# A new order table for the same 2,900 operations of a fused convolution and linear-attention kernel

## The chip, the cores and the metric

The kernel runs on one core of a Trainium2 chip. The metric is the device time of one execution in microseconds (us), the median of a few runs. Its engines are TensorE (PE in the profile, with its weight loads as PEld), VectorE (DVE), ScalarE (ACT), GpSimd (POOL) and SyncE (SP). SP issues all data transfers of this kernel.

## The reference, cut to what matters

Two independent layers are computed and laid side by side in the last axis. `u` and `x` are (1, 2048, 576).

```python
# left half: a state-space convolution per channel, N = 128 states
dt = exp(log_dt); A = -exp(log_A_real) + 1j * A_imag; C = (C_real + 1j * C_imag) * dt[:, None]
K  = 2 * einsum("dn,dnl->dl", C, exp((A * dt[:, None])[:, :, None] * arange(2048))).real
a  = irfft(rfft(u_t, 4096) * rfft(K, 4096))[:, :, :2048] (transposed back) + u * D_skip
# right half: linear attention, 32 heads of 18
q, k, v = split(x @ wqkv)
phi(z)  = concat(softmax(z @ w_phi), softmax(-(z @ w_phi)))      # per head
num = phi(q) @ (phi(k)^T v);  den = phi(q) . sum(phi(k))
b = (num / (den + 1e-6)) @ wo
out = concat([a, b], -1)
```

## The kernel before, in words

The kernel is written in two layers. `body` first describes the work: each call of `op` records one operation with its engine, a cost, the function that emits its instructions, and the buffers that it reads and writes. 2,900 operations are recorded; 486 of them are PE blocks of 1 to 32 matmuls, 366 are transfers. Then `Plan.run(ORDER)` goes through a table of numbers and emits the operations in the table's order. The table is the only thing that decides in which order each engine meets its instructions; nothing reorders them on the chip. An engine works through its own instructions in that order and stops at the first one whose inputs, or whose buffer, are not there yet.

One entry of the table is an operation's number with marks behind it. `1494` is operation 1494. `376*` says that the operation goes to its second engine: copies from PSUM can go to ACT or DVE, and many SBUF-to-SBUF operations to POOL or DVE. `/3/0/5` are the slots that its new buffers take: 8 PSUM banks (`ps`), 14 large buffers (`zi`, `ac`, `x9`, `e`, `ks`, `E`), 19 rows (`v1`, `o`, `ot`, `yo`, `ub`, `kb`, `us2`, `zo`, `ff`, `fT`, `mx`), 7 small ones, 2 each of `pi`, `mg`, `cs`. A buffer waits until the slot's former user has been read. `!` puts a tiny ACTIVATE in front, which loads the activation table early. `35+28` puts 28 matmuls with zeros ahead of operation 35.

The work itself, by the names in the functions:

- `fold` and `whole` (L504 to L536) prepare weights: `wh` is the rounded part, `wl` the rest, so that three products of reduced precision make up one in f32.
- `key_tile(t)`, 16 tiles of 128 rows: `load_x` (L547, L467) splits x into a rounded part and a rest, three `gemm`s of 14 matmuls give phi's argument and v, `softmax` (L590 to L607) works on DVE, POOL and ACT, and 32 small matmuls add to phi(k)^T v.
- `query_tile(t)`, 16 tiles: two `gemm`s, `softmax`, transposes (L705), the division by `den` (L724), transposes (L735, L736) and two `gemm`s with `wo`.
- `u_first(k)`, 16 steps, and `product(p, half)`, 16 steps, and `last`, 16 steps: the Fourier transform of u, its product with that of K, and the way back, all as small matmuls that use the array in tiles of 32 or 64 rows and columns (`ub,ff`, `kb,ff`, `ac,ff`, `zi,w`).
- `params(blk)`, 6 blocks (L843 to L886): angles, on vectors of 96 per partition, mostly on DVE. `phases` (L904, L908): chains of integer additions on POOL. `waves` (L918 to L926): sines on ACT. `group(g)`, 36 groups: exponentials (L942, L949), products on DVE (L953 to L959), 32 small matmuls (`E,cs`), then copies and sums into `ks`. `k_first` turns each quarter of the groups into `zi` and writes it to DRAM; before it, L471 adds D_skip to `ks` (`ks<-ks,dsk`).

L452 is the line of the helper that issues almost all matmuls, L457 and L460 are the copies from PSUM, L467 and L471 the binary operations, so one line stands for many uses, and the names of tiles tell them apart. `copy("any", ...)` is what makes an ACT-or-DVE choice possible:

```python
op(("act", "dve"), (c_act(n), c_dve(n)), lambda e: act.activation(dst(), src(), AF.Copy) if e == "act" else dve.tensor_copy(dst(), src()), r=r, w=w)
```

All stages overlap: key tiles, u steps and the first groups share the first 200 us, query tiles, groups and the first half of the products the next 150 us, and the last 150 us hold the other products, `last` and the remaining query tiles.

## Time and profile before

| what | value |
| --- | --- |
| runs | 515.43, 518.12, 514.73 us; median 515.43 us |
| the profiled execution | 511.75 us, of which 510.0 us are the span from the first to the last instruction |
| granted TensorE clock | 0.999 |
| transfers | 114.67 MB by 366 issues on SP, 225 GB/s of HBM over the span |
| ACT_TABLE_LOAD | 41, of 1.28 us each |

The profile takes one execution. A row of a timeline reads: start and length in us, engine, source line, instruction, tiles written and read, shape, count, and in brackets the engine's idle time before it with what ended it. A row of groups ends with the group's busy time, the mean length of one in ns, and the idle time before. Lengths of neighbouring DVE instructions overlap a little, since the end of one lies beside the start of the next.

### The profile page before, as it was taken

The page shows a single profiled execution, that of the slowest core. Times are in us where ns is not written, and L with a number is a line of the kernel's source. Part 1 is how long each engine was busy: PE and PEld are TensorE (multiplying, and loading weights), DVE is VectorE, ACT ScalarE, POOL GpSimd, SP SyncE. Part 2 cuts the span into 40 slices and gives each one's busy share as a digit, 9 for nine tenths or more (in the row PEclk, how much of TensorE's full clock was granted, in tenths as well). Part 3 has the DMA queues.
Part 4 walks back from the last instruction along what each step waited for, and adds up shares of the span by engine and source line. Part 5 has one row for each costly group of instructions (what it writes and reads, how often), then busy time and mean ns, then how long its engine had stood idle before and what let it go on. Part 6 is the DMA issues. An engine that isn't in the chain of part 4 may idle for free.

```text
span 510.0 us, 20296 instructions
## 1 busy us (share of the span) xinstructions
PE 496.6 (97%) x8436; PEld 412.6 (81%) x8436; DVE 457.5 (90%) x1013; ACT 396.8 (78%) x683; POOL 334.2 (66%) x403
## 2 busy tenths in 40 slices
PE   7999999999999999899999999999999999999996
PEld 7799888999998879697887866776788886667976
DVE  4999999999899999999999999998989879789774
ACT  4699787999879989979989889899896445454331
POOL 1645697788987997995994569796554455634400
PEclk9999999999999999999999999999999999999999
DMA  7985947715137586781687965468986997998797
GB/s 212 333 294 178 330 143 252 235 57 170 59 121 254 149 257 207 212 275 58 211 239 255 286 180 181 147 219 272 293 269 213 347 274 219 321 311 295 260 314 193
DMA packets 80511, 115.95 MB, mean 227 GB/s; under 512 B 12452, under 2 KB 57636, under 8 KB 80420
## 3 DMA queue, kind: packets, MB, share of 16 engines
q1 hardware_dynamic: 80420, 114.67, 71.1%
q8 instruction: 66, 1.08, 0.9%
q14 instruction: 25, 0.20, 0.1%
HBM read 65.63 MB, written 49.01 MB: 225 GB/s over the span
## 4 chain that ended last, share of the span: by engine, by line
PE 80%; DVE 7%; ACT 6%; POOL 2%; DMA 2%; issue 2%; SPq 0%; POOLq 0%; DVEq 0%
PE ps L452 75%; PE ps L705 3%; PE ps L735 2%; POOL cs L908 1%; ACT cs L918 1%; DVE E L471 1%; DMA xd<-x 1%; DMA ub<-dram 1%; ACT e L598 1%; DMA fT<-in_wphi_dram 1%; POOL o L601 1%; DVE wl L520 1%; DVE e L467 0%; DVE zi L457 0%; DVE small L602 0%
## 5 line engine op out<-in xcount | busy, mean ns | idle before, releaser
L452 PE MATMUL ps<-wh,x 128*128 128x288 f32 (+2 forms) x1008 | 240.2, 318 | 1.0 <-ACT wh L519 0.4
L452 PEld LDWEIGHTS ps<-wh,x 128*128 128x128 f32 x1008 | 173.0, 188 | 11.8 <-issue 2.8
L452 PE MATMUL ps<-wl,x 128*128 128x288 f32 (+2 forms) x560 | 175.0, 313 | 0.0
L452 PEld LDWEIGHTS ps<-wl,x 128*128 128x128 f32 x560 | 105.3, 188 | 1.2
L908 POOL TENSOR_TENSOR cs<-cs,pi 128x64 int32<-128x64 int32 (+4 forms) x90 | 91.9, 1022 | 5.5
L601 POOL TENSOR_TENSOR o<-e 128x576 f32<-128x576 f32 x32 | 42.4, 1330 | 28.8 <-ACT e L598 22.3
L467 POOL TENSOR_TENSOR E<-v,cs 128x512 f32<-128x512 f32 x31 | 39.5, 1290 | 15.5 <-ACT v L949 12.6
L471 DVE TENSOR_TENSOR ac<-us,ps 128x576 f32<-128x576 f32 x64 | 44.8, 747 | 3.5 <-PE ps L452 2.5
L953 DVE TENSOR_TENSOR cs<-ps,cs 128x1024 f32<-128x1024 f32 x36 | 43.7, 1214 | 2.8 <-ACT ps L942 2.4
L942 ACT ACTIVATE ps<-ps 128x512 f32<-128x512 f32 x72 | 41.6, 591 | 5.1 <-PE ps L452 4.8
L598 ACT ACTIVATE e<-e 128x1152 f32<-128x1152 f32 x32 | 37.4, 1168 | 7.0 <-POOL e L467 4.8
L452 PEld LDWEIGHTS ps<-E,cs 128*32 128x32 f32 x2304 | 34.3, 110 | 10.5 <-issue 5.7
L467 POOL TENSOR_TENSOR e<-small,e 128x576 f32<-128x576 f32 x27 | 31.7, 1173 | 15.7 <-DVE small L467 10.7
L452 PE MATMUL ps<-sel,mg 128*128 128x512 f32 x108 | 40.4, 439 | 1.4 <-DVE e L471 1.0
L452 PE MATMUL ps<-E,cs 128*32 128x64 f32 x2304 | 40.1, 220 | 1.4 <-issue 0.6
L926 ACT ACTIVATE cs<-cs,hp 128x1024 f32<-128x1024 f32 x36 | 40.4, 1141 | 0.0
L925 ACT ACTIVATE cs<-cs 128x1024 f32<-128x1024 int32 x36 | 37.0, 1054 | 0.3
L918 ACT ACTIVATE cs<-cs 128x2048 f32<-128x2048 int32 x18 | 34.4, 1912 | 2.6 <-POOL cs L908 2.5
L457 ACT ACTIVATE zi<-ps 128x288 f32<-128x288 f32 x79 | 28.1, 414 | 8.4 <-PE ps L452 8.4
L467 POOL TENSOR_TENSOR e<-e,small 128x576 f32<-128x576 f32 x25 | 29.7, 1189 | 7.3 <-DVE small L467 6.6
L890 POOL TENSOR_TENSOR pi<-pi 128x192 int32<-128x192 int32 (+1 forms) x42 | 20.0, 486 | 18.9 <-DVE pi L886 16.8
L467 POOL TENSOR_TENSOR ac<-ac 128x288 f32<-128x288 f32 x24 | 19.2, 825 | 18.8 <-DVE ac L471 8.8
(146 smaller groups left out, 1050.0 us busy)
## 6 DMA issues: line engine op xcount, KB each, us to landing
dram<-zi SPq DMA_DIRECT2D x32, 288.0 KB, 4.8
xd<-x SPq DMA_DIRECT2D x16, 576.0 KB, 4.7
dram<-zi SPq DMA_DIRECT2D x16, 576.0 KB, 5.2
x<-xd SPq DMA_DIRECT2D x16, 576.0 KB, 5.6
kb<-dram SPq DMA_DIRECT2D x32, 288.0 KB, 4.6
ub<-dram SPq DMA_DIRECT2D x32, 288.0 KB, 6.2
dram<-zo SPq DMA_DIRECT2D x32, 288.0 KB, 4.4
zi<-dram SPq DMA_DIRECT2D x16, 576.0 KB, 8.8
```

Of the source, the lines that this page charges most:

```text
L452: pe.matmul(o, l, r, start=start, stop=stop, skip_group_check=skip)
L457: op(("act", "dve"), (c_act(n), c_dve(n)), lambda e: act.activation(dst(), src(), AF.Copy) if e == "act" else dve.tensor_copy(dst(), src() ...
L467: op(eng, [c_dve(n[0]) if e == "dve" else c_pool(n[1]) for e in eng], lambda e: (dve if e == "dve" else pool).tensor_tensor(dst(), a(), b( ...
L471: op(eng, c_dve(n) if eng == "dve" else c_pool(n), lambda: e.tensor_tensor(dst(), a(), b(), op=alu), r=r, w=w, with_=with_, lock=eng == "p ...
L598: op("act", c_act(1152) + 40, lambda: act.activation(e.t, e.t, AF.Exp), r=[e], w=[e], table="exp")
L601: op("pool", c_pool(517), lambda: pool.tensor_tensor(pair.t, e.t[:, :, :, 0:9], e.t[:, :, :, 9:18], op=ALU.add), r=[e], w=[pair], lock=True)
L908: op("pool", c_add(4 * n * W), lambda n=n, j=j: pool.tensor_tensor(x()[:, :, :, n:2 * n], x()[:, :, :, 0:n], pi.t[:, j:j + 2, gs].bitcast( ...
L918: op(("act", "dve"), (c_act(n) + 45, c_dve(n)), lambda e: act.activation(cs.t[:, 0], x(), AF.Abs) if e == "act" else dve.scalar_tensor_ten ...
L925: op("act", c_act(64 * W) + 150, lambda at=at: act.activation(at(1), at(1).bitcast(I32), AF.Sin, scale=TURN), r=[cs], w=[sine], with_=[cs] ...
L926: op("act", c_act(64 * W) + 225, lambda at=at: act.activation(at(0), at(0), AF.Sin, scale=-TURN, bias=hp.t), r=[cs, hp, sine], w=[both], w ...
L942: op("act", c_act(512) + 12, lambda: act.activation(ps.t, ps.t, AF.Exp), r=[ps], w=[ps], table="exp")
L953: op("dve", c_dve(64 * W), lambda: dve.tensor_tensor(F(), both(M.t), F(), op=ALU.mult), r=[M, ready], w=[long], with_=[cs])
```

## The change

The table `ORDER` is replaced by another one. It holds the same 2,900 operations, and nothing else of the kernel differs. The new table is one line shorter, so that every line behind it has a number that is lower by one (L452 becomes L451). The first two lines of each:

```diff
 ORDER = """
-180/0 33 0/0 1 1353 3 1358 2 1360 1362 72/1 1361 1366 396/2 1365 1368 1367/3 1369 1370 1371 1372 4/4 35+28/0 1359 1373
-1374 126/5 1377 1363/0 1364 1375 1376 1378 1379/3 1380 1381 34/1 5/0 7/2 10 19/6 36 12/1 374/7 37 26/2 6/3 8 40/3 20/4
...
+2847 2848 2850 847 2880/2/0/6 1112 2849 1086 2868 2892 2873/7/5/7 2861 2869 2871 2881* 2882 2870 2883 2885 2894/3/4/14
+2895 2874 2852/0/1/2 1116/5/4 2884 2853* 2896 1117/10 849/1 2875 848/2 1118 1008 1119 1120 2876 2878 2897 850/6 2854
+2855 2898 2877 2856 2862 2863 2899 1121/3 2857 851 852 2864 1123/16 1122/1 1124 1125
```

In words, the new table is the former one with most entries moved by a few places. PE's blocks keep their places within a few blocks; the 28 matmuls with zeros stay. 172 operations change their engine: 63 from ACT to DVE, 57 from DVE to ACT, 27 from POOL to DVE, 25 from DVE to POOL. DVE's instructions go from 1,013 to 1,021, ACT's operations from 636 to 630, POOL's from 399 to 397. The changes of activation table in ACT's order go from 41 to 43, the early loads (`!`) from 6 to 8. The slots are dealt out anew.

Three places show it. The first is DVE near the start, where the weights' rests (`wl`) are made while the first key tile's x is split (`x<-zo,x`: the tile in f32 less its rounded part). Before:

```order
L622 MEMSET ps 128x288
L520 TENSOR_TENSOR wl<-ps,wh 128x4x126
L467 TENSOR_TENSOR x_216<-zo,x_216 128x512
L520 TENSOR_TENSOR wl<-ps,wh 128x126 x4
L520 TENSOR_TENSOR wl<-ps,wh 128x4x126
L520 TENSOR_TENSOR wl<-ps,wh 128x72
L536 TENSOR_TENSOR wl<-zi,wh 128x5x192
```

And now:

```order
L519 TENSOR_TENSOR wl<-ps,wh 128x4x126
L519 TENSOR_TENSOR wl<-ps,wh 128x126
L466 TENSOR_TENSOR x_240<-zo,x_240 128x512
L466 TENSOR_TENSOR x_240<-zo,x_240 64x128
L519 TENSOR_TENSOR wl<-ps,wh 128x4x126
L519 TENSOR_TENSOR wl<-ps,wh 128x126
L535 TENSOR_TENSOR wl<-zi,wh 128x5x192
```

The subtraction of 64x128, which stood on POOL, now stands on DVE ahead of the last two `wl`.

The second place is DVE around the addition of D_skip to the second quarter's `ks` (L471 before, L470 now; 128x36), behind which PE's second `k_first` can start. `ax`, `ay`, `mx`, `mn`, `cim` belong to `params`, the other `ks` to groups. Before:

```order
L859 SCALAR_TENSOR_TENSOR mx<-ax,ay 128x96
L471 TENSOR_TENSOR mn<-ax,ay 128x96
L471 TENSOR_TENSOR ay<-ay,ax 128x96
L457 COPY ks<-ps 128x32x4
L471 TENSOR_TENSOR x_4010<-ps,x_4010 64x128
L471 TENSOR_TENSOR ks<-ps,ks 128x32x4 x3
L471 TENSOR_TENSOR ks<-ks,dsk 128x36
L471 TENSOR_TENSOR ks<-ps,ks 128x32x4
L871 RECIPROCAL mx<-mx 128x96
```

And now:

```order
L855 TENSOR_SCALAR cim<-cim 128x96
L470 TENSOR_TENSOR ks<-ps,ks 128x32x4
L470 TENSOR_TENSOR ay<-ay,ax 128x96
L470 TENSOR_TENSOR ks<-ps,ks 128x32x4
L589 TENSOR_REDUCE small<-ps 128x16
L470 TENSOR_TENSOR ks<-ps,ks 128x32x4 x2
L470 TENSOR_TENSOR ks<-ks,dsk 128x36
L470 TENSOR_TENSOR ks<-ps,ks 128x32x4
L870 RECIPROCAL mx<-mx 128x96
```

Ahead of that addition stood 472 DVE instructions before, and 487 stand there now, while 196 PE blocks stand ahead of that `k_first` in both. The row of `mn`, which stood just ahead, now stands elsewhere, and a maximum of a softmax (`small<-ps`) has come in.

The third place is PE late in the program, where step `p1` of a product (`ub,ff`, 64x32 tiles of the array), its `p2` (`kb,ff`, 32x32 tiles) and a query tile's transposes (`ident,e`, the whole array) meet. Before:

```order
L452 MATMUL ps<-wl,x_7743 128x288
L452 MATMUL ps<-ub,ff 32x288 x16
L452 MATMUL ps<-kb,ff 32x288 x16
L705 MATMUL ps<-ident,e 128x128 x5
L452 MATMUL ps<-zi,w_432 64x288 x4
```

And now:

```order
L451 MATMUL ps<-wl,x_7750 128x288
L451 MATMUL ps<-ub,ff 32x288 x16
L704 MATMUL ps<-ident,e 128x128
L451 MATMUL ps<-kb,ff 32x288 x16
L704 MATMUL ps<-ident,e 128x128 x4
L451 MATMUL ps<-zi,w_2188 64x288 x4
```

One transpose moved between the two steps, so that the array's tiling changes once more often. Over the whole program it changes 219 times between neighbouring PE blocks before and 229 times now; behind the first 326 blocks it is 77 and 83.

## The prediction

> **What bounds the kernel now.** I read the windows by stage first, then the timelines of DVE and PE at the two borders between the stages, then the groups by line for prices. The columns of the windows are PE, PEld, DVE, ACT, POOL, the clock, the DMA share and GB/s.

> ```profile
> 20.00:231.00 211.00, 207.72 (x3444) 184.67 (x3442) 204.92 (x443) 188.70 (x300) 171.20 (x209) 1.00 0.63 200
> 231.00:348.00 117.00, 114.90 (x2224) 89.01 (x2225) 109.58 (x248) 106.05 (x178) 86.95 (x97) 1.00 0.66 205
> 348.00:510.00 162.00, 157.36 (x2670) 123.25 (x2668) 130.72 (x293) 91.03 (x184) 70.11 (x78) 1.00 0.86 274
> ```

> PE looks full everywhere, but its busy time includes ends that are modelled. DVE tells the stages apart. From 20 to 231 us it is busy 204.92 of 211 us, idle for 6.1 (2.9%); from 231 to 348 it is idle for 7.4 of 117 (6.3%); behind that for 31.3 of 162. So the first stage is DVE's, the second nearly so, and the third is PE's. I chose the borders where PE waits for DVE. The first is the second `k_first`, in DVE's and PE's timelines:

> ```profile
> 230.44 0.49 DVE L471 TENSOR_TENSOR ks<-ks,dsk 128x36 f32<-128x36 f32 x1
> 230.85 0.28 DVE L471 TENSOR_TENSOR ks<-ps,ks 128x128 f32<-128x128 f32 x1
> 231.05 0.74 DVE L871 RECIPROCAL mx<-mx 128x96 f32<-128x96 f32 x1
> 230.98 0.77 PE L452 MATMUL ps<-ks,w 32*128 32x288 f32 x8 [0.36 <-DVE ks L471]
> ```

> The addition of D_skip ends at 230.93, and PE, idle by then, starts 0.05 us later. No row of DVE here has an idle time in brackets: the addition came when DVE came to it, and DVE had 472 instructions ahead of it. The second border is the block `E,cs` of the sixteenth group:

> ```profile
> 347.63 0.68 DVE L959 SCALAR_TENSOR_TENSOR E<-ps,cs 128x512 f32<-128x512 f32 x1
> 348.37 1.46 PE L452 MATMUL ps<-E,cs 128*32 128x64 f32 x64
> ```

> The last `E` ends at 348.31, PE starts at 348.37, and 720 instructions of DVE stand ahead. What PE can do by those two points is thus set by the time of DVE's instructions ahead of them plus DVE's idle time. That is what I count for the new order.

> **DVE's additional work ahead of the borders.** In the new order 487 DVE instructions stand ahead of the first border, 15 more. Order alone moves one more ahead than behind, of lengths that cancel to nothing. The other 14 come from changed engines. Before that point 25 copies go from ACT to DVE and 16 back, and 17 operations from POOL to DVE and 12 back. The groups' mean lengths (in ns, the second number behind the bar) give their price:

> ```profile
> L457 DVE COPY zi<-ps 128x288 f32<-128x288 f32 x49 | 20.8, 451 | 4.4 <-PE ps L452 3.6 <-POOL small L467 0.4
> L457 DVE COPY v<-ps 128x180 f32<-128x180 f32 (+1 forms) x6 | 2.5, 411 | 0.1
> L457 DVE COPY ks<-ps 128x128 f32<-128x128 f32 x13 | 3.5, 278 | 0.8 <-PE ps L452 0.8
> L467 DVE TENSOR_TENSOR x<-zo,x 128x512 fp32r<-128x512 f32 (+1 forms) x20 | 13.4, 676 | 0.4 <-ACT x L547 0.2
> L467 DVE TENSOR_TENSOR kb<-ub 128x288 f32<-128x288 f32 x14 | 7.0, 503 | 0.0
> L467 DVE TENSOR_TENSOR small<-small 128x32 f32<-128x32 f32 x20 | 4.7, 240 | 0.1
> L467 DVE TENSOR_TENSOR e<-e,small 128x576 f32<-128x576 f32 x7 | 5.4, 773 | 0.0
> ```

> By net count: 2 copies of 128x288 at 0.451 (one into `zi`, one into `e`) 0.90; 5 copies of v at 0.411, 2.06; 2 copies of `ks` at 0.278, 0.56; 2 of `x<-zo,x` at 0.676, 1.35; 1 `kb` at 0.503; 3 `small` at 0.240, 0.72; and one `e<-e,small` less, −0.77. Together 5.3. The rows of DVE overlap: the one at 230.85 lasts 0.28, to 231.13, and the next starts at 231.05. At 0.07 to 0.08 for each of 14 that takes off 1.0, which leaves **4.3**. By the second border it is 737 instructions instead of 720, two more, small ones at 0.24, or 0.5: **+4.8 us** of DVE work ahead of it. The subtraction that the new order puts ahead of the last two `wl` in the head is one of the `x<-zo,x`, so it is counted; the nearest PE row is

> ```profile
> 15.36 0.41 PE L452 MATMUL ps<-wh,x 128*128 128x378 f32 x1 [0.37 <-ACT wh L519]
> ```

> and shows PE's first gemm waiting for these weights already.

> **DVE's idle time.** The order between the borders is new as well, and with it the 7.4 us of idle time. An order that hands DVE more may also leave it fewer gaps. The bounds are none absorbed and all: 7.4 here and 6.1 ahead of 231, 13.5. I take the value that the trace shows DVE to reach over a long stage, the 2.9% from 20 to 231 us: 2.9% of 117 is 3.4, so 7.4 − 3.4 = **4.0** are absorbed. Ahead of 231 nothing is, since that stage is at the 2.9% already.

> **Waits inside DVE's busy time.** Some of that time isn't work:

> ```profile
> 6.31 0.26 DVE L471 TENSOR_TENSOR mn<-mn,mx 128x96 f32<-128x96 f32 x1
> 232.38 1.98 DVE L471 TENSOR_TENSOR mn<-mn,mx 128x96 f32<-128x96 f32 x1
> 229.06 5.18 POOL L908 TENSOR_TENSOR cs<-cs,pi 128x64 int32<-128x64 int32 x5
> L471 DVE TENSOR_TENSOR mn<-mn,mx 128x96 f32<-128x96 f32 x6 | 3.2, 539 | 0.0
> 10.12 0.46 DVE L471 TENSOR_TENSOR pi<-pi,ot 128x288 f32<-128x288 f32 x1
> L471 DVE TENSOR_TENSOR pi<-pi,ot 128x288 f32<-128x288 f32 x6 | 4.1, 686 | 0.0
> 5.24 0.25 DVE L859 SCALAR_TENSOR_TENSOR mx<-ax,ay 128x96 f32<-128x96 f32 x1
> L859 DVE SCALAR_TENSOR_TENSOR mx<-ax,ay 128x96 f32<-128x96 f32 x6 | 2.6, 431 | 0.0
> L859 DVE SCALAR_TENSOR_TENSOR pi<-th,dt 128x96 f32<-128x96 f32 x6 | 2.6, 438 | 0.0
> ```

> The same product takes 0.26 us at 6.31 and 1.98 at 232.38, where it ends at 234.36, just behind POOL's chain of additions, which ends at 234.24: DVE stands still until POOL has finished. Over four kinds of six each the excess is 6 × (0.539 − 0.26) = 1.7, 6 × (0.686 − 0.46) = 1.4, 6 × (0.431 − 0.25) = 1.1 and, at the same 0.25, 6 × (0.438 − 0.25) = 1.1, together 5.3. Two more kinds of two SBUF operands can be set beside rows of the same shape that read one operand from PSUM:

> ```profile
> L467 DVE TENSOR_TENSOR x<-zo,x 128x512 fp32r<-128x512 f32 x14 | 10.2, 734 | 0.3 <-ACT x L547 0.2
> 227.39 0.68 DVE L471 TENSOR_TENSOR x<-ps,x 128x512 fp32r<-128x512 f32 x1
> L467 DVE TENSOR_TENSOR x<-zo,x 64x128 fp32r<-64x128 f32 x6 | 3.2, 540 | 0.1
> 229.51 0.29 DVE L471 TENSOR_TENSOR x<-ps,x 64x128 fp32r<-64x128 f32 x1 [0.22 <-ACT x L460]
> L471 DVE TENSOR_TENSOR yo<-ps,yo 128x288 f32<-128x288 f32 x32 | 14.3, 452 | 3.4 <-ACT yo L457 2.6 <-DMA zi<-dram 0.2
> ```

> That is 14 × (0.734 − 0.68) + 6 × (0.540 − 0.29) = 2.3 for `x<-zo,x`, and 14 × (0.503 − 0.452) = 0.7 for `kb`: 8.3 with the four. For the products of the softmax no such row is at hand; I estimate the whole at about 10. Which DVE row meets which POOL row is drawn anew by the new order: the bounds are all 10 gone, or a few more waits. I take no change, since POOL has as many additions to do and DVE as many such rows.

> [...]

> **PE's tilings and the rest.** Behind 348 us PE is the bound, and there each change of the array's tiling costs.

> ```profile
> 429.34 1.19 PE L452 MATMUL ps<-zi,w 128*64 128x288 f32 x8
> 430.46 0.77 PE L452 MATMUL ps<-ac,ff 32*32 32x288 f32 x32
> 432.03 1.17 PE L452 MATMUL ps<-zi,w 128*64 128x288 f32 x8
> 433.03 0.73 PE L452 MATMUL ps<-kvb,fT 128*64 128x76 f32 x16
> ```

> Eight `zi,w` behind whole-array transposes take 1.12 us from start to next start; eight behind and ahead of `kvb,fT`, of the same 128*64 tiles, take 1.00. So a change is worth 0.12; between unlike sizes I take 0.15. Six more behind that border make **+0.9**. The four ahead of it lie beside DVE's queue and cost nothing there, or 0.6 where it gives way. Two more table loads stand in ACT's order:

> ```profile
> L925 ACT ACT_TABLE_LOAD x16 | 20.5, 1283 | 0.3
> ```

> At 1.283 each they fit into the 22 us that ACT is idle between 20 and 231 us (188.70 busy of 211); without that cover they cost 2.6. The transfers are the same 366, and neither border's wait ends on one, so they are put at nothing.

> **The sum.** +4.8 (DVE's work) − 4.0 (its idle time) + 0.9 (tilings) = **+1.7 us**. The profiled execution took 511.75 us, of which 510.0 are the span; so 513.45 by that execution. The runs' median stands 3.68 above the profiled one, and 513.45 + 3.68 = **517.1**. With 0 to 7.4 absorbed it lies between 521.1 and 513.7, its own range.

> **The rivals.** A measurement of this kernel can tell about 1% from no change, 5.2 us either way, or 510.3 to 520.6.

> *Nothing but shifts.* The borders' time is made by chains through several engines, and DVE's additional rows fall where it would have waited: 515.4. For it: PE's blocks keep their places, and the totals of DVE differ by 8 of 1,013. Against it: 15 rows are concentrated ahead of 231 us, where there are only 6.1 us of idle time to fill.

> *Faster: DVE's waits behind POOL mostly vanish.* If POOL's work and DVE's rows with two SBUF inputs stand apart in time in the new order, the 8 us of the six kinds are gained: 4.8 − 8 − 4.0 + 0.9 = −6.3, or **509.1**; with all idle time of the second stage absorbed too, 505.7. For it: the one wait at 232.38 is as large as the whole net change of the forecast, and the row that stood next to the border (`mn`) has moved. Against it: POOL is busy for 171.20 of the 211 us, so there is little room to stand apart.

> *Slower: DVE gives nothing back.* DVE stays as idle as now, 4.8 + 0.9 = +5.7, and the five operations that DVE takes from POOL on balance ahead of 231 us wait behind additions of

> ```profile
> L908 POOL TENSOR_TENSOR cs<-cs,pi 128x64 int32<-128x64 int32 (+4 forms) x90 | 91.9, 1022 | 5.5
> ```

> a third of 1.022 each on average, 5 × 0.34 = 1.7: +7.4, or **522.8**. It decides from where less than about 0.5 us of idle time is absorbed, since 5.7 − 0.5 passes 5.2. For it: DVE is at 97.1% for 211 us, and 9 of its 14 additional rows come from ACT, which is the less busy of the two. Against it: DVE's gaps at the second border's stage are more than twice as dense as ahead of it, so some should close.

> [...]

> **How the numbers follow.** Forecast 0.31, only shifts 0.12, faster 0.32, slower 0.25. The forecast leads the shifts because the count of DVE's rows is certain, and the faster case is nearly as likely because half of the waits' price hangs on which rows meet. Faster by over 1% is 0.32, within it 0.31 + 0.12 = 0.43, slower 0.25. The range reaches from the faster rival with the second stage's gaps closed, 505.7, to a little above the slower one, 523.5; a tenth is left out on either side.

> **What would show it.** Right: DVE busy for at least 97% up to the second `k_first`, whose block `ks,w` starts at 234 to 236 instead of 230.98 us; the block `E,cs` of the sixteenth group within 1 us of 349.2; DVE idle for 3 to 4 us between the two; the rest of the span 1 us longer than 161.6. Wrong: the second `k_first` starts ahead of 231 us although more DVE rows stand ahead of it. Then the means of `mn<-mn,mx`, `pi<-pi,ot` and `mx<-ax,ay` say whether it was the waits behind POOL: near 0.26, 0.46 and 0.25 for the faster rival, unchanged where DVE's gaps closed instead. A slower kernel with DVE as idle as before is the slower rival; one with DVE idler, and PE waiting for ACT or a transfer, is none of these.

## The result, and the profile after

The new table takes 533.88 us (median of four runs, 531.16 to 535.02) where the former one, beside it on the same chip, takes 515.08 (four runs, 512.65 to 518.12): a ratio of 1.0354, interval 1.0284 to 1.0424. The kernel is slower, by 18.8 us. That lies outside the predicted range, 505.7 to 523.5. The profiled execution took 532.99 us, of which 531.2 are the span. The one of before, 511.75, is 3.3 us faster than the median of its kernel, and this one 0.9, so some 2.4 us of the differences between the two traces below are the spread of executions. Where a run took over 1.5% longer than the fastest of the same kernel, it is left out of the figures.

The first page, of the kernel after: how much of the span each engine is busy, the clock in 40 slices, and the chain that ended last.

```profile
span 531.2 us, 20259 instructions
PE 504.6 (95%) x8436; PEld 418.8 (79%) x8436; DVE 457.7 (86%) x1021; ACT 398.7 (75%) x681; POOL 334.9 (63%) x401
PEclk9989999999999999989998999999999999999999
PE 70%; DVE 11%; ACT 7%; DMA 5%; issue 4%; POOL 1%; SPq 1%; DVEq 0%; POOLq 0%; ACTq 0%
```

The same four of before:

```profile
span 510.0 us, 20296 instructions
PE 496.6 (97%) x8436; PEld 412.6 (81%) x8436; DVE 457.5 (90%) x1013; ACT 396.8 (78%) x683; POOL 334.2 (66%) x403
PEclk9999999999999999999999999999999999999999
PE 80%; DVE 7%; ACT 6%; POOL 2%; DMA 2%; issue 2%; SPq 0%; POOLq 0%; DVEq 0%
```

DVE's busy time is the same, 457.7 us after 457.5. PE stands still for 531.2 − 504.6 = 26.6 us instead of 13.4, which is 13.2 of the 21.2 us that the span grew, and its rows last 8.0 us longer in all. In the chain, issue and transfers have taken 9% where they had 4%. Three slices of PEclk fall below 9; before, none does.

Next the windows, cut first at the former borders and then at the new ones (columns as in the prediction):

```profile
20.00:231.00 211.00, 202.54 (x3274) 179.02 (x3276) 198.63 (x435) 178.81 (x278) 163.94 (x198) 0.99 0.60 188
231.00:348.00 117.00, 111.92 (x2083) 90.04 (x2087) 105.50 (x241) 99.98 (x170) 80.63 (x90) 0.97 0.63 194
20.00:244.00 224.00, 212.86 (x3445) 188.66 (x3444) 207.61 (x459) 186.58 (x291) 170.45 (x205) 0.98 0.58 184
244.00:364.60 120.60, 117.57 (x2227) 91.13 (x2225) 112.36 (x251) 108.31 (x179) 86.78 (x96) 0.99 0.66 204
```

Every engine does less in the same 211 us: PE 3,274 matmuls instead of 3,444, DVE 198.63 us of work instead of 204.92, ACT and POOL less as well. No engine has become fuller; all of them wait more.

The borders, in DVE's and PE's timelines:

```profile
243.04 0.18 DVE L470 TENSOR_TENSOR ks<-ks,dsk 128x36 f32<-128x36 f32 x1
244.24 1.01 PE L451 MATMUL ps<-ks,w 32*128 32x288 f32 x12
```

The second `k_first` starts at 244.24 (before 230.98, forecast 234 to 236). The sixteenth group's `E,cs` starts at 364.64 (before 348.37, forecast 349.2), and the rest of the span is 166.6 (before 161.6, forecast 162.6). So 13.3 us are lost ahead of the first border, 3.0 between the two, 5.0 behind. At the first border DVE's addition ends at 243.22, 12.3 us later than before, and PE comes to the block 1.0 us after that, out of a gemm and without a wait: there it is no longer DVE that holds PE up.

The rows of DVE that the prediction named as waits behind POOL:

```profile
L470 DVE TENSOR_TENSOR mn<-mn,mx 128x96 f32<-128x96 f32 x6 | 1.8, 294 | 0.0
L470 DVE TENSOR_TENSOR pi<-pi,ot 128x288 f32<-128x288 f32 x6 | 2.7, 452 | 0.1
L858 DVE SCALAR_TENSOR_TENSOR mx<-ax,ay 128x96 f32<-128x96 f32 x6 | 1.4, 242 | 1.2 <-ACT ax L848 1.2
L858 DVE SCALAR_TENSOR_TENSOR pi<-th,dt 128x96 f32<-128x96 f32 x6 | 3.0, 498 | 0.0
```

Three of the four are down at their bare lengths (0.294, 0.452, 0.242 us against the 0.26, 0.46 and 0.25 that were to show the faster rival). That rival's mechanism came about on these rows, and the kernel is slower all the same.

### The profile page after: what moved, and what is told of

Read it like the earlier page. It is cut to its first block, busy times and chain, and to the rows that moved or that the text cites. A ratio compares the mean times of both kernels' runs of the same rounds, so it can differ in the third digit from the quotient of the medians.

```text
span 531.2 us, 20259 instructions
## 1 busy us (share of the span) xinstructions
PE 504.6 (95%) x8436; PEld 418.8 (79%) x8436; DVE 457.7 (86%) x1021; ACT 398.7 (75%) x681; POOL 334.9 (63%) x401
## 3 DMA queue, kind: packets, MB, share of 16 engines
q8 instruction: 66, 1.08, 0.8%
## 4 chain that ended last, share of the span: by engine, by line
PE 70%; DVE 11%; ACT 7%; DMA 5%; issue 4%; POOL 1%; SPq 1%; DVEq 0%; POOLq 0%; ACTq 0%
PE ps L451 65%; PE ps L704 3%; DMA zo<-in_xT_dram 1%; PE ps L734 1%; DMA e<-in_wkT_dram 1%; DMA kb<-dram 1%; DVE cs L952 1%; ACT cs L917 1%; ACT ps L941 1%; DVE E L470 1%; DVE E L956 1%; DVE small L589 1%; DMA ks<-in_mag_dram 1%; DVE ac L470 1%; ACT cs L924 1%
## 5 line engine op out<-in xcount | busy, mean ns | idle before, releaser
L451 PE MATMUL ps<-wh,x 128*128 128x288 f32 (+2 forms) x1008 | 242.0, 320 | 1.8 <-DVE E L956 0.7
L451 PEld LDWEIGHTS ps<-wh,x 128*128 128x128 f32 x1008 | 175.1, 190 | 11.8 <-issue 2.3
L451 PE MATMUL ps<-wl,x 128*128 128x288 f32 (+2 forms) x560 | 176.3, 315 | 0.0
L451 PEld LDWEIGHTS ps<-wl,x 128*128 128x128 f32 x560 | 106.6, 190 | 1.3
L907 POOL TENSOR_TENSOR cs<-cs,pi 128x64 int32<-128x64 int32 (+4 forms) x90 | 89.2, 991 | 5.7
L466 POOL TENSOR_TENSOR E<-v,cs 128x512 f32<-128x512 f32 x32 | 41.0, 1298 | 26.5 <-ACT v L948 26.5
L941 ACT ACTIVATE ps<-ps 128x512 f32<-128x512 f32 x72 | 41.8, 588 | 13.8 <-PE ps L451 13.3
L470 DVE TENSOR_TENSOR ac<-us,ps 128x576 f32<-128x576 f32 x64 | 44.5, 746 | 7.3 <-PE ps L451 5.2
L451 PE MATMUL ps<-E,cs 128*32 128x64 f32 x2304 | 41.9, 224 | 8.4 <-issue 4.8
L451 PEld LDWEIGHTS ps<-E,cs 128*32 128x32 f32 x2304 | 35.7, 112 | 17.7 <-issue 10.3
L451 PE MATMUL ps<-sel,mg 128*128 128x512 f32 x108 | 42.9, 453 | 0.9 <-DVE e L470 0.3
L925 ACT ACTIVATE cs<-cs,hp 128x1024 f32<-128x1024 f32 x36 | 40.6, 1141 | 0.0
L466 POOL TENSOR_TENSOR e<-e,small 128x576 f32<-128x576 f32 x27 | 32.2, 1192 | 9.3 <-DVE small L466 8.5
L466 POOL TENSOR_TENSOR ac<-ac 128x288 f32<-128x288 f32 x27 | 21.2, 811 | 20.7 <-DVE ac L470 16.3
L889 POOL TENSOR_TENSOR pi<-pi 128x192 int32<-128x192 int32 (+1 forms) x42 | 19.5, 474 | 23.0 <-ACT wh L518 10.9
L456 ACT ACTIVATE zi<-ps 128x288 f32<-128x288 f32 x71 | 25.9, 413 | 10.2 <-PE ps L451 9.9
```

The source lines that it names most:

```text
L451: pe.matmul(o, l, r, start=start, stop=stop, skip_group_check=skip)
L466: op(eng, [c_dve(n[0]) if e == "dve" else c_pool(n[1]) for e in eng], lambda e: (dve if e == "dve" else pool).tensor_tensor(dst(), a(), b( ...
L470: op(eng, c_dve(n) if eng == "dve" else c_pool(n), lambda: e.tensor_tensor(dst(), a(), b(), op=alu), r=r, w=w, with_=with_, lock=eng == "p ...
L907: op("pool", c_add(4 * n * W), lambda n=n, j=j: pool.tensor_tensor(x()[:, :, :, n:2 * n], x()[:, :, :, 0:n], pi.t[:, j:j + 2, gs].bitcast( ...
L925: op("act", c_act(64 * W) + 225, lambda at=at: act.activation(at(0), at(0), AF.Sin, scale=-TURN, bias=hp.t), r=[cs, hp, sine], w=[both], w ...
L941: op("act", c_act(512) + 12, lambda: act.activation(ps.t, ps.t, AF.Exp), r=[ps], w=[ps], table="exp")
```

## Where PE stands still

The waits of PE summed by what ended them, from 24 us on, after and then before (total, times, longest):

```profile
PE ps L451 <- issue: 4.8, 3, 2.7
PE ps L451 <- DVE cs L952: 1.8, 2, 1.4
PE ps L451 <- DVE e L470: 1.6, 3, 1.0
PE ps L451 <- ACT zi L456: 1.4, 3, 0.5
PE ps L451 <- DVE E L466: 1.3, 1, 1.3
```

```profile
PE ps L452 <- DVE e L471: 1.3, 3, 0.5
PE ps L705 <- POOL e L467: 1.0, 1, 1.0
PE ps L452 <- issue: 0.6, 1, 0.6
```

The largest term after has no engine behind it: issue, 4.8 us in three waits. Two of them, and the wait for DVE's `E`, in PE's timeline:

```profile
196.04 0.80 PE L451 MATMUL ps<-E,cs 128*32 128x64 f32 x41
198.67 1.43 PE L451 MATMUL ps<-E,cs 128*32 128x64 f32 x87 [1.83 <-issue]
...
230.93 0.64 PE L451 MATMUL ps<-E,cs 128*32 128x64 f32 x29
234.25 1.21 PE L451 MATMUL ps<-E,cs 128*32 128x64 f32 x35 [2.68 <-issue]
...
278.60 1.65 PE L451 MATMUL ps<-E,cs 128*32 128x64 f32 x56 [1.28 <-DVE E L466]
```

**Issue.** The block at 230.93 breaks off after 29 of its 64 matmuls, though all of its inputs are there, since matmuls of one block share them. What PE lacked there, read from the order in time, is instructions: the trace holds the DMA packets of a queue of their own (`instruction`, 66 packets in 1.08 MB, 16 KB each). The packet that belongs to the first place came at 196.1 us and took 1.05, and PE went on 1.49 us behind its end; the second came at 231.9, took 0.98, and PE went on 1.41 behind it. In the 18 traces of this document PE has 53 waits of over 0.3 us at issue, and 52 of them end 1.1 to 1.7 us behind the end of such a packet, the four of this trace and that of before 1.29 to 1.61 us behind it. What may have delayed it is read from SP's timeline:

```profile
222.19 1.26 SPq L777 DMA_DIRECT2D dram<-zi  x2
223.63 1.67 SPq L557 DMA_DIRECT2D x<-xd  x2
225.39 1.09 SPq L777 DMA_DIRECT2D dram<-zi  x2
226.54 0.59 SPq L832 DMA_DIRECT2D mg<-gd  x1
```

SP issued nothing from 218.0 to 222.2 us, because its next store waited 4.1 us for ACT's copy into `zi`, and then ten transfers within 7.6 us; the DMA share, 0.04 from 220 to 222, is 1.04 from 230 to 232. The packet, the 26th, began when PE had started 6,794 matmuls and weight loads; before, the 26th began at 6,633, a count that PE reached here at 227.1 us, 4.8 us earlier. How long these waits are differs between executions: the same table, run again (`new_again`), has 0.89 us at the first place and 1.88 at the second.

**The clock.** Behind PE's wait of 2.68 us, at 234.4, behind the one for `E`, at 278.7, and near 30 us (though not behind the wait of 1.83) the granted clock is halved for 3.4 us:

```profile
234.40:237.80 3.40, 3.40 (x44) 3.14 (x38) 2.31 (x5) 1.58 (x3) 0.38 (x1) 0.50 0.40 116
278.70:282.10 3.40, 3.40 (x65) 3.23 (x66) 3.37 (x7) 1.53 (x4) 0.96 (x1) 0.51 0.77 224
```

PE counts as busy all that time, but its gemms go at 0.24 us apiece (235.98, then 236.22) instead of 0.13. From the clock of 0.50 I estimate one such stretch at 3.4 × 0.5 = 1.7 us where PE has work. Before, the clock is 1.00 from 10.9 us to 509.

What went ahead of it can be read from all 18 traces together. In each of them the clock changed only at whole multiples of 3.413 us from its first change: here 234.36 − 29.56 = 204.80 is 60 times that, and 278.74 − 234.36 = 44.38 is 13 times. So I summed PE's idle time over these stretches of 3.413 us, from 14 to 500 us. Where it was over 1.83 us, half clock followed every time (11 stretches); where it was under 1.2, it never did; in between it followed 11 stretches and not 35 others (stretches at half clock themselves aside). In the new table's trace it followed those with 1.52, 1.90 and 2.68 us of idle time and not those with 1.45 and 1.83, the second of which holds the wait of 1.83, and no other stretch has over 0.88. In the trace of before the most is 0.96, and half clock followed none.

**What this sums to.** I compared the 486 PE blocks, each by the time from the end of the block before it to its own, with the lower quartile of such times over blocks of the same kind and tiling change in both traces:

```
             floor   excess   in blocks over 2 us   1 to 2   0.5 to 1   under 0.5
before       475.8     30.1          5.7 (1 block)     3.6        8.7        12.1
after        477.0     49.2         17.8 (5 blocks)    5.0        9.5        16.9
```

The floor grew by 1.2 us. Of the 19.1 that the excess grew, 12.1 lie in blocks that lost over 2 us each: 1.2 at the very start (6.9 us after 5.7, where the first transfer is awaited) and 10.9 at four places that lost nothing like it before: 2.6 at 30 us, in the head; 2.1 at 199; 3.4 at 235; 2.8 at 280. The other 7.0 lie in many blocks that lost less. They need not all be the table's: `former_burst`, whose median is that of the former table, ends 3.3 us behind this trace of before.

## The experiments

The tables of all experiments are written with the same marks. Unless said otherwise the operations are the same 2,900, and where the slots didn't fit, they were dealt out anew. "Of before" is always the former table's run on the same chip. Two ways of thinking are set against each other again and again: that each loss is local, so that a wait taken away shows in the total, and that something further on gives the gain back.

**Order or engines.** The change does two things at once: it reorders, and it moves 172 operations to their other engine. Both were tried alone. `order_only` has the new order with the former engines (lines of the new table, shortened):

```diff
-377* 40/3 29 31 46/1 30 32 ... 268* 269* 1287/10 51/2 379/6
+377 40/3 29 31 46/1 30 32 ... 268* 269 1287/10 51/2 379/6
```

> The new order and its slots, with every operation on the engine that it had before. Theory A (the loss is a handful of long waits of PE that the new order makes by coincidence: PE's instructions fetched late at 197 and 232 us, DVE behind POOL at 275, a late start at 27 us; three of them are followed by 3.4 us at half clock): most of the loss stays, +8 to +15 us over the kernel before, though single waits may fall away. Rival B (DVE's additional rows by changed engines are the cause): at most +4. Rival C (any shift of this kernel costs as much, whichever part is taken): about as slow as the whole change, +16 or more.

`engines_only` has the former order with the new engines, the same edit the other way round:

```diff
-... 376* 377 17 28/1 11 24 25
+... 376 377* 17 28/1 11 24 25
```

> The former order and slots, with the 172 operations on their new engines. Theory A: DVE has 4 to 5 us more to do ahead of the second k_first and some chains are longer, but no long wait of PE: +3 to +8 us. Rival B: +12 us or more, DVE at over 97% up to the second k_first. Rival C: +12 us or more too, but with DVE idle for more than 14 us up to there, and PE waits of over 1.5 us in places where the new table has none.

Measured: 562.39 against 516.01, ratio 1.0897 [1.0843, 1.0950], and 553.02, ratio 1.0726 [1.0664, 1.0788]. That is +46.4 and +37.0, each two to two and a half times as bad as the whole, and far above what a handful of long waits was to make of them (+8 to +15, +3 to +8). So DVE's additional rows by themselves are not the price of the change, and the rows that go to POOL and ACT not its gain; each order fits its own engines. On average a mismatched operation cost (46.4 − 18.8) / 172 = 0.16 us against the new order with its own engines, or 37.0 / 172 = 0.22 against the former. The losses lie all along: in both traces 20 blocks of PE lose 1 to 2 us each, 26 to 28 us together, against 3.6 before (counted as in the table above).

**Which stretch.** `new_head` goes through the new table to entry 1424 (some 254 us in) and then does the rest in the former order; `new_tail` does the former order to entry 1352 (some 236 us in) and then the new one.

```diff
@@ new_head @@
 ... (new table, entries 1 to 1424)
+... (the remaining operations, in the order and with the engines of the former table)
```

> The new table up to its 1,424th entry (209 of 486 PE blocks, 256 us in its trace), with its engines, and the remaining entries in the former order and on the former engines; 16 buffers take another slot, since the former one is still held. Theory D (each stretch loses what its own rows cost, and PE, full behind it, cannot take it up again): the new table is 12.7 us behind at that block, the rest runs as before, so +11 to +15 us over the kernel before, 526 to 531. Theory E (a table fits only the times at which its own rows arrive, and any seam or shift costs tens of us, as in the two kernels with half the change): over 535. Theory F (the loss up to there is waiting that the former tail takes up again in its gaps): under 522.

> The former table up to its 1,352nd entry (197 of 486 PE blocks, 232 us), then the remaining entries in the new order and on the new engines; 19 buffers take another slot. Theory D: the new table loses 20.4 - 12.8 = 7.6 us behind that block, so +6 to +10 us over the kernel before, 521 to 526. Theory E: over 530. Theory F: about 533, since the tail is what costs.

Measured: 532.32 against 517.85, +14.5, ratio 1.0276 [1.0205, 1.0347]; and 528.22, +10.4, ratio 1.0202 [1.0116, 1.0287]. The first lies within the +11 to +15 of Theory D, the second just above its +6 to +10, and neither fits E or F. In the trace of the whole, PE was 12.7 us behind the former table's at the last block of the new head and 20.4 at the end. In `new_head`'s own it was 10.5 behind at that block; it lost 8.1 more in the 24 blocks behind the seam of the two orders, up to 281 us, and 3.1 in all the rest. In `new_tail`'s it lost 3.4 us up to 170 us, in the part that is still the former table, where `former_burst` loses 2.6 as well; then 4.1 in a single block at the seam, where PE waits 3.51 us for one of DVE's copies, and 7.9 in the rest. So each half of the new table loses by itself, and the other half doesn't give it back. How much each loses isn't shown: the two sum up to 24.9 us, more than the 18.8 of the whole, and the seams, which the whole doesn't have, are part of that.

**The late instructions.** `fetch_both` moves eight transfers on SP, so that the burst from 222 to 230 us is drawn apart:

```diff
-... 1009/6 521 ... 525/11 486/2 ... 697/5 1751/3 ... 853/12 1158 ... 1175 647 ... 1276 1764 ... 892/6 1961 ... 1275 1862*
+... 1750 1275 1276 1175 853/12 697/5 1306 ... 619/2 525/11 ... 1325 1009/6 ... 1865 892/6 ...
```

> The new table with eight transfers moved on SP's queue: six from the burst at 222 to 230 us (five ahead of it, into the time in which no transfer runs, one behind), two from the burst at 189 to 196 us to behind it. Operations, engines and slots else as in the new table. Theory A: PE's two waits without a releaser (1.83 us at 197, 2.68 us at 232) end when a 16-KB packet of the instruction queue lands, and that packet came late because transfers stood ahead of it; with fewer of them it comes in time, both waits go, and so does the half clock behind the second one (3.4 us at half, 1.7 lost): 6 us less than the new table, about 528. Rival: the waits have another cause (a semaphore that the trace does not show), they stay where they are in the program, and the time stays within 2 us of the new table's.

Measured: 532.14 against 516.01, ratio 1.0303 [1.0259, 1.0348]. PE in its timeline:

```profile
227.95 0.64 PE L451 MATMUL ps<-E,cs 128*32 128x64 f32 x29
230.06 0.75 PE L451 MATMUL ps<-E,cs 128*32 128x64 f32 x35 [1.47 <-issue]
359.10 2.12 PE L451 MATMUL ps<-ub,ff 64*32 64x288 f32 x28 [0.67 <-DMA ub<-dram]
```

The wait at 197 us is gone and the second one, behind the very same 29th matmul, is shorter by 1.2 us, with no half clock behind it: at the 198th block PE is 5.7 us ahead of the new table's trace, of which about 2 come from the head, where this execution had no half clock near 30 us. But the lead falls from 4.8 us at the 323rd block to 2.2 at the 360th: around 359 us a load of `ub` comes late, with a half clock behind that. In the total nothing is left that can be told apart. Nor does this trace show that the moves took the waits away. With the new table's own transfers the first wait is missing too in `clock_kept` and `new_head`, and the second is 1.33 to 2.68 us long in six traces. With 853 moved further on, as in `all_moved` and `three_places` below, neither wait is there.

To show that late instructions cost time by themselves, `former_pile` piles two stores ahead of such a packet in the former table, where nothing else differs:

```diff
-... 2406/18 2509 2347/2 ... 2563/4 2153 2579/17 ... 2307 2465 2421
+... 2406/18 2509 2465 2153 2347/2 ... 2563/4 2579/17 ... 2307 2421
```

> The kernel before, with two stores (zo of product 2 and zi of the third k_first, 288 KB each, whose data is ready at 331 us) issued on SP's queue at 346 us instead of at 367 and 355. Nothing else is moved. The 16 engines are busy throughout from 342 to 350 us in the trace of before, and the instruction packet that PE asks for near 348.5 us lands at 352.1. If late fetches make PE's waits without a releaser: 576 KB at 345 GB/s put the packet 1.7 us later, it lands near 353.8, PE stands still at the end of the instructions it holds (near 353.2 us in the former trace) until 1.4 us behind the landing, about 2 us, with no releaser in the record; the kernel is up to 2 us slower, or up to 4 with a half clock. If not: no wait of over 0.7 us without a releaser at 350 to 358 us.

Measured: 517.70 against 515.66, ratio 1.0055 [1.0021, 1.0089], so +2.0. A block of 40 matmuls that ran through in 1.86 us before (`kvb,fT` at 352.39) breaks off after 23:

```profile
353.90 1.02 PE L452 MATMUL ps<-kvb,fT 128*64 128x76 f32 x23
356.92 1.45 PE L452 MATMUL ps<-kvb,fT 128*64 128x19 f32 x17 [2.01 <-issue]
```

Its packet came at 354.4, took 1.14 us, and PE went on 1.42 behind its end; from 356.7 on the clock is at half for 3.4 us. With the two stores ahead of it, the packet landed 1.6 us behind the start of that block, where it had landed at 352.1, 0.3 ahead of it, and PE stood still for 2.01 us: a wait like the one at 232 us of the new table, made at will. A first attempt, `former_burst`, moved two loads of the former table ahead of a third:

```diff
-2032 2515 2087 2247/1 2553 950/1/3 2398/12 2498/15 2033 ...
+2032 2515 2087 2398/12 2498/15 2247/1 2553 950/1/3 2033 ...
```

> The kernel before, with two loads (320 and 288 KB, ff and kb of later products, not needed before 324 us) issued on SP's queue at 289 us ahead of a small load, instead of at 293 to 294 us. Nothing else is moved. In its trace, the instruction packet that PE asks for near 289.4 us lands at 293.7, 0.8 us ahead of the latest start by which PE had gone on in other places, and the transfers ahead of it keep the 16 engines busy throughout. If late fetches are what makes PE's waits without a releaser: the 608 KB take about 2 us more, the packet lands near 295.5 and PE stands still for 1 to 3 us in the block E,cs at 295 us, with no releaser, until 1.4 us behind the landing; the kernel is 1 to 4 us slower than before. If not: no such wait, and the time within 1 us of before.

Measured: 515.59 against 516.53, ratio 0.9987 [0.9944, 1.0030]. It made no burst: the loads waited on SP for their buffers until 294.1, and PE's wait for issue there stayed at 0.51 us (0.56 before). It decides nothing.

**The wait behind POOL.** At 271.61 to 276.31 POOL works through four additions of `phases`, and DVE's two `E<-v,cs` of 274.88 take 3.67 us where they took 0.68 and 0.70 before. `lock_moved` puts the last of these additions (1998, of 2.04 us) behind a sum of the softmax (865):

```diff
-1998 2224 1943 1947 ... 865/12 1946 1942/18
+2224 1943 1947 ... 865/12 1998 1946 1942/18
```

> The new table with one entry moved: the last and longest addition on POOL of the phases of group 11 (128x1024, 2.04 us) goes behind the sum of the softmax that followed it. Theory A: the two products E<-v,cs on DVE, 1.98 and 1.77 us in the new table against 0.69 undisturbed, no longer wait for POOL, or for 1.3 us less; PE's wait at 276 to 278.6 us shrinks by 1 to 2 us and the half clock behind it (1.7 lost) goes: 2 to 4 us less than the new table, 530 to 532. Rival: PE's time lost there is taken up again later, since PE isn't the bound everywhere: within 1 us of the new table.

Measured: 532.69 against 516.01, ratio 1.0313 [1.0263, 1.0362]. The two rows took 2.41 us, and PE's wait for them fell as it should:

```profile
278.62 0.99 PE L451 MATMUL ps<-E,cs 128*32 128x64 f32 x56 [0.70 <-DVE E L466]
```

From 1.28 to 0.70, and no half clock behind it: PE, 15.9 us behind the former table at that place in the new one, was 14.8 behind here, although it had come there 1.3 us later, with 6.8 us at half clock from 233.7 on. By the 306th block it was level with the new table again.

**The head.** `head_moved` puts two steps of the magnitudes (1332 on DVE, 1333 on ACT), which stand ahead of what PE waits for near 28 us, nine entries later:

```diff
-1332 1333 1516 53 1330/6 ... 43/7 384 388*/2
+1516 53 1330/6 ... 43/7 384 1332 1333 388*/2
```

> The new table with two entries moved by some ten places near the start: the sum ac<-ac,ld on DVE and the exponential behind it on ACT (L800, with its table load) go behind the softmax difference on DVE and the copy zi<-ps on ACT that PE's second Fourier step needs. In the new table ACT stands 3.8 us in that exponential, waiting for DVE's sum, with the copy behind it, and PE waits 1.02 and 0.51 us. Theory D: PE is 1 to 1.5 us earlier at 35 us, and where the half clock at 30 us (it was there in the new table and in the run with the moved addition, 3.9 to 4.2 us behind at that place, and not in the two others, 2.2 behind) stays away, 2 us more; at the end 531 to 532.5. Theory F: within 1 us of the new table.

Measured: 535.10 against 517.85, ratio 1.0357 [1.0274, 1.0441]. PE's wait of 1.02 for `e` fell to 0.28, and one of 2.54 for ACT's `zi` came at 33.97 in its place, with a half clock behind it. `head_old` takes the first 201 entries from the former table and the rest from the new one:

```diff
 ... (former table, entries 1 to 201)
+... (the remaining operations, in the order and with the engines of the new table)
```

> The first 201 entries of the former table (20 PE blocks, 37 us), the rest in the new order on the new engines; 2 buffers take another slot. Theory D: PE starts as in the former kernel, the 2.2 to 4.2 us that the new table loses by 35 us are saved and stay saved: 530 to 532 where before is 515. Theory F: taken up again by the same places behind it, within 1 us of the new table (534).

Measured: 534.18 against 516.57, ratio 1.0351 [1.0306, 1.0397]. PE was 1.1 us behind at the 18th block instead of 4.2, but 6.3 behind at the 27th: there it waited 2.5 us for a transfer (`mg<-gd`), with a half clock from 56.3 on. A gain of 3 us was lost 20 us later.

**The clock by itself.** `clock_kept` is the new table with 14 matmuls of zeros ahead of the block that waits for `E` (1933), so that PE has something to do meanwhile:

```diff
-1998 2224 1943 1947 1933/3 1934
+1998 2224 1943 1947 1933+14/3 1934
```

> The new table with 14 matmuls with zeros (0.11 us each by the 28 at the start) ahead of the block E,cs of group 9, at which PE waits at 276 to 278.6 us for DVE's two products, with a half clock of 3.4 us behind it. Operations, order, engines and slots as in the new table. Theory A (PE's idle time triggers the half clock, and each costs PE about 1.7 us): no half clock behind this place, and PE is 1 to 2 us earlier behind 282 us, relative to its place ahead of the block, than in the new table; the other half clocks stay. Rival (the half clock comes by other causes, or its time is hidden, since PE waits for others anyway): the half clock stays, or PE is no earlier at 290 us.

Measured: 530.95 against 516.57, ratio 1.0277 [1.0227, 1.0326]. In its trace:

```profile
272.16 1.59 PE L227 MATMUL ps<-ident,zero 128*32 128x256 bf16 x13
274.45 0.99 PE L451 MATMUL ps<-E,cs 128*32 128x64 f32 x56 [0.47 <-DVE E L466]
276.00:280.00 4.00, 4.00 (x95) 3.74 (x97) 3.90 (x12) 3.98 (x5) 2.28 (x2) 1.00 0.94 308
```

The clock stays at 1.00, and over this place PE loses 1.0 us on the former table instead of 2.1, with the zero matmuls' own 1.59 us mostly inside the wait. But that the zeros kept the clock up isn't shown by this, since in `new_again`, the same table without them, it stays up as well, behind the very same wait:

```profile
277.83 0.99 PE L451 MATMUL ps<-E,cs 128*32 128x64 f32 x56 [1.28 <-DVE E L466]
276.00:284.00 8.00, 6.44 (x187) 5.80 (x187) 7.90 (x17) 5.52 (x9) 4.03 (x3) 1.00 0.84 264
```

There PE loses 0.9 us. So about 1.1 us is what the half clock costs at this place, and the zeros gained nothing that an execution without them doesn't show. The execution of `clock_kept`, with the same table up to there, had no half clock at 30 and 234 us either, which shows how much one execution differs from the next.

**All of it at once.** `all_moved` joins the moves of the head, of the lock and of the transfers, `repaired` the old head with the moves of lock and transfers, `three_places` the moves of lock and transfers with the zero matmuls; `new_again` is the new table once more, beside the last of them. The moves of transfers are those of `fetch_both`, but with 853 behind 1909 and 697 where it was.

```diff
@@ all_moved @@
-1332 1333 1516 53 ... 853/12 1158 ... 1998 2224 1943
+... 384 1332 1333 388*/2 ... 1909 853/12 652 ... 865/12 1998 1946
```

> The new table with three sets of moves at once: the two entries near the start, the last addition of the phases of group 11 on POOL behind the sum of the softmax, and transfers moved on SP's queue (three stores of zi ahead of the burst at 222 us, two loads of x behind its stores or behind the burst, two loads behind the burst at 190 us). Theory D: the named waits add up, 1.3 at 28 us, 1.8 at 197, 2.7 at 232, 1.3 to 1.9 at 277, with up to three half clocks of 1.7 each: 5 to 9 us less than the new table, 525 to 529. Theory F: what one of them gives, another place takes back, as at 355 us in the kernel with the moved transfers; 531 to 533.

> As the run with the former first 201 entries, and with the moves of transfers on SP's queue and of POOL's last addition as in the run with all moves (without the moves near the start). Theory D: the named places together, the start 2.2 to 4.2, the two late fetches 4.5, the products behind POOL 1.3 to 1.9, and their half clocks: 9 to 12 us less than the new table, 522 to 525 where before is 515; what is left, 7 to 10 us, lies in places of under 1 us each. Theory F: no better than the run with all moves (+10.9 over before).

> The new table with the moves of transfers on SP's queue and of POOL's last addition, as in the run with all moves, and the 14 matmuls with zeros ahead of group 9's block E,cs; the start is the new table's own. Theory D (what is saved at these places stays saved): 4.5 of fetches, 1 to 2 behind POOL, one to two half clocks of 1.7 make 6 to 9 us less than the new table on the same chip. Theory F (taken back by the places behind them): under 3 us less.

> The new table once more, unchanged. It should be 1.03 to 1.04 times before again; its profile shows which long waits belong to the table (those at 28, 197 and 277 us, which came in every run of it) and which to one execution (the length of the one at 232 us, 2.7, 1.5 and 2.4 us so far, and two or three half clocks).

Measured: `all_moved` 528.88 against 517.85, ratio 1.0228 [1.0157, 1.0299]; `repaired` 529.90 against 516.57, ratio 1.0265 [1.0213, 1.0317]; `three_places` 530.39 and `new_again` 529.79, both against 516.53, ratios 1.0269 [1.0200, 1.0338] and 1.0231 [1.0143, 1.0318]. The new table measured again stands at +13.3 instead of +18.8, with runs from 528.04 to 531.82. Against that, none of the repairs can be told from the new table. In the trace of `three_places` PE is 1.6 to 3.4 us ahead of `new_again` from the 190th block to the end (16.8 us behind the former table instead of 18.8); the total doesn't show it.

**Is DVE the bound at all?** The prediction built on that. `former_apart` moves eight operations of the former table, so that DVE's rows meet POOL's less often:

```diff
-... 2047 1858 ... 2048 1960 701 1857* 702/10 ... 1883/1 1734 ... 70* 1348 ... 1705/9 1243 ... 331 205* ... 1536 229/12
+... 1857* 2047 2048 702/10 ... 524 1883/1 1884 ... 1201* 70* ... 355 1705/9 ... 331 80* ... 230/3 1536
```

> The kernel before, with eight entries moved a few places so that DVE's rows with two SBUF operands no longer stand where POOL works in its trace: mn<-mn,mx (1.98 us at 232.4) and the arctangent behind it go behind four rows that read PSUM or one operand; pi<-th,dt at 195.8 and what follows on ACT behind three; a reciprocal's product at 48.0, mx<-ax,ay at 77.5, x<-zo,x at 153.2 and pi<-pi,ot at 58.2 behind one to three each. By the former trace that takes 4.9 us of waiting out of DVE's first 235 us. Theory G (the premise of the prediction: DVE's time sets PE's there): the second k_first starts 3 to 5 us earlier than 231, and the kernel is 2 to 5 us faster than before, 510 to 513 where before is 515. Theory H (DVE, PE and the others hold one another up in turn; time that one of them gains turns into its idle time): within 1.5 us of before, with DVE idle for 3 to 5 us more ahead of the second k_first.

Measured: 517.33 against 516.57 in five rounds, ratio 1.0014 [0.9986, 1.0041]. Ahead of the second `k_first` DVE's time behind POOL fell from 12.1 to 9.8 us, and its idle time rose from 13.8 to 17.5 (both sums as in the table of the next section). PE was 1.3 us ahead at the 63rd to 108th block, but the second `k_first` started 1.8 us later, at 232.80. At the border:

```profile
232.16 0.21 DVE L471 TENSOR_TENSOR ks<-ks,dsk 128x36 f32<-128x36 f32 x1
232.80 1.25 PE L452 MATMUL ps<-ks,w 32*128 32x288 f32 x16
```

PE came 0.43 us after the addition had ended and had no wait, where before it had waited 0.36 us for it. That it came later than before is within what executions differ: in `former_burst`, `former_pile` and `new_tail`, which have the former table up to there, that block starts at 232.29 to 234.34, and PE waits 0.36 to 0.39 us for the addition in each. DVE's idle time, though, is 14.3 to 15.3 us in those, less than here. The moves were to take 4.9 us off DVE and took 2.3, and a total shorter by 2.3 would be a ratio of 0.9955, below the interval. So what DVE spent less went into DVE's waiting, not into PE's progress.

## Why the prediction was wrong, point by point

I took each DVE instruction ahead of a border apart into its undisturbed length (the shortest tenth of its kind in both traces), what it lasted beyond that (beside POOL), and DVE's idle time before it:

```
ahead of the second k_first   instructions   undisturbed   beyond   idle
before                              473          236.0       12.1   13.8
after                               488          240.5        8.6   25.0
former_apart                        473          236.0        9.8   17.5
```

These are single executions. In the other traces of the former table the idle time is 14.3 to 15.3 us, in those of the new table and its repairs 19.9 to 25.3, so the size of its growth is uncertain, its sign isn't.

- *DVE's additional work*: right. 240.5 − 236.0 = 4.5 us against 4.3 by the sum; by the second border 364.6 − 359.7 = 4.9 against 4.8.
- *Waits inside DVE's busy time, no change*: wrong in size, to the good. They fell by 3.5 us. Such a wait shows in the new trace as well, 3.67 us at 274.88 beside POOL's additions against 1.38 for the two rows before. There PE came for that result and waited 1.28 us; but the 2.3 us that `former_apart` took out of such waits brought nothing in the total.
- *DVE's idle time, 4.0 absorbed*: the step that failed. It didn't shrink, it grew by 25.0 − 13.8 = 11.2 us ahead of the first border and by 12.1 ahead of the second (33.3 instead of 21.2). Work, waits and idle time together are 4.5 − 3.5 + 11.2 = 12.2; the addition moved by 12.3 and PE's block by 13.3. The prediction took idle time as room that additional work fills, and bounded it by none absorbed and all, so that no growth was allowed for. It is where DVE itself waits, in its gaps of over 0.15 us for ACT (8.0 us before, 13.5 after) and PE (2.2 and 7.9), and a new order makes its own.
- *What bounds the first stage*: the premise beneath it failed too. That DVE was busy for 97.1% and that PE came for its result at the border was read as "DVE's time sets PE's"; `former_apart` took time off DVE, and neither the border nor the end came earlier; in the new kernel PE comes to the border 1.0 us after DVE's addition. That all four engines are coupled there within a few us, so that each loses what one loses, is what I make of it; no run shows it by itself.
- *The late instructions and the clock*: not in the sum at all. Before, one wait of 0.56 us at issue and no half clock stood in the trace (the four other traces of the former table have one more such wait, of 0.86 to 1.02 us, at 164 to 168 us); after, 4.8 us and three stretches at half clock. That stores piled up ahead made the instructions late, with a wait of 2.01 us, is shown by `former_pile`; that half clock followed PE's idle time (each time over 1.83 us in a stretch, never under 1.2), by all traces together; what one cost, about 1.1 us at 279, by two executions of the same table. That the four places make up 10.9 us of the loss is worked out from the blocks of one trace, and no run recovered them in the total.
- *Tilings*: right in size, +1.2 us of floor over all blocks against 0.9, though behind the first 326 blocks the changes are 77 and 81, four more and not six, so that the sum's own term would be 0.6. No run shows a change between unlike sizes by itself; its 0.15 was the author's estimate, above the 0.12 read from the rows. *ACT's table loads*: no run tests them. They fit into ACT's idle time, 37.4 us from 20 to 244, but in the head one load at 26.89 stands behind 3.81 us of ACT's idle time, just ahead of PE's wait for `zi`.
- *Transfers put at nothing*: wrong. They are the same 366, but SP stood at a store that waited and then issued ten at once, and the instructions came late behind them. That the burst made them late there is read from the order in time; `former_pile` shows the like at another place.
- *Of the rivals* none was it. The prediction's last sentence names the case, though, a slower kernel in which DVE is idler and PE waits for ACT or a transfer, but gave it no chance of its own.

Two theories made on the way fell as well. That the moved operations are the cost fell with `order_only` and `engines_only`. That taking away the named waits one by one gains their price in the total fell with `fetch_both`, `lock_moved`, `head_old`, `repaired` and `three_places`: most did at their place what they should, and the total stayed within what runs of the new table differ among themselves. What remains open is the cause of the rest, about 7 us in many small losses that no one place explains and of which some are the spread of executions, and how much of the four long ones would be gained if all of them could be taken away at once. No version tried beats the former table.

## What to carry to other kernels

Where four engines are all busy for 80 to 97%, the fullest one is not thereby the bound: test it by taking time off it, and see whether the border comes earlier, before building a sum on its work. A new order's price lies less in its work, which can be counted (4.5 us, right within 0.2), than in the waits that it makes new; look, for each long stretch of the transfer queue's order, for a store that will wait with a burst of transfers behind it. The one long wait of PE that was seen with and without a half clock behind it cost about 1.1 us more with it, at its place (279 us). Look at a second trace of each kernel before pricing a single wait: here the wait at the same place took 2.68 us in one execution and 1.88 in another.
